# Attention and squared-ReLU feed-forward in one kernel: where the two bursts of a head pair stand among the up products

## The chip, the cores and the metric

The kernel runs on one core of a Trainium2 chip. The metric is the device time of one execution in microseconds, the median of several runs; less is better. Before the change the median of 3 runs is 394.03 us (393.51 to 394.4).

A core has five engines that run side by side and meet only at semaphores. TensorE (PE) multiplies matrices into the eight banks of its result memory (PSUM), VectorE (DVE) and ScalarE (ACT) read those banks, GpSimd (POOL) works between buffers and issues loads, SyncE (SP) issues stores and transposing transfers. In the profile, PEld is the loading of a matmul's stationary operand.

## The reference

Eight batches of 384 tokens pass through attention with 16 query heads and 4 key heads of width 64, then through a feed-forward layer of 1024 to 2048 to 1024 with a squared ReLU:

```python
k = np.repeat(k, group, axis=1)
v = np.repeat(v, group, axis=1)
scores = scale * np.matmul(q, k.transpose(0, 1, 3, 2))
attn = np.exp(scores - max)
attn = attn / (np.sum(attn, axis=-1, keepdims=True) + 1e-09)
attn_out = np.matmul(attn, v)
...
x = attn_out.transpose(0, 2, 1, 3).reshape(B * S, H * D)
h = np.maximum(x @ w_in, 0.0)
out = h * h @ w_out
```

## The kernel before

The kernel is written as a planner in Python. A `Recorder` keeps, for each engine, a clock made from costs written into the code, and appends operations one after the other; at the end `emit` (L116) writes each engine's instructions in that order, with semaphore waits where one engine needs another. So the order on each engine is fixed when the program is built: the planner's clock decides only who goes first, and the chip then waits wherever the planner's clock was too early.

Batches 0 and 1 go through a first loop (L1776 to L1928). Batches 2 to 7 go through the second loop (L1931 to L2014), which the change touches. Per batch b it has two stages.

**Up products.** x times w_in, done as Strassen products (`strassen`, L868): seven products of half size instead of eight. The work is cut into pieces of eight matmuls, four on each half of the array's rows (`zipped`, L836; the matmuls carry L927). There are 28 product tiles, two halves each, so some 57 pieces per batch. Results leave four of the eight banks (4 to 7) by DVE or ACT: copies (L903, L906), additions to an earlier tile (L911), the tile with the ReLU (L898), then the ReLU and square (L812, L820, L824). A bank is used again by the fourth tile after.

**Down products.** The squares times w_out, Strassen again over pairs of row blocks (`stream`, L967; matmuls L971). They are long for odd b (27 us) and short for even b (12 to 14 us). Their results are scaled and added by DVE and ACT (L1126, L1127, L1134) and one addition by POOL (L1169). The first pieces of batch b+1's up products overlap with the last of batch b's down products.

**Attention of the next batch among them.** While batch b is multiplied, batch b+1's attention is done in the gaps of the order, in the other four banks, which are used in two pairs, (0, 1) and (2, 3):

- A score burst, called "sc" (`burst_small`, L464): 2 or 4 matmuls (L471) into one bank pair; ACT then takes the exponential of the whole pair (L481) into a ring of 6 unit slots. A batch has 12 units and 18 score bursts. A slot can be taken again only when the two head pairs that read it are done (L1967).
- A head pair c (8 per batch, `av_halves`, L525): two bursts of 18 matmuls (L539). The first burst ("av") takes a bank pair and holds it, the second ("av2") adds the other halves to it and must not start before the first has ended (`after=(lead,)`, L547). Then DVE reads the pair: a reciprocal (L552), the product into o_sb (L554), and later a maximum (L1506). After every second head pair SP issues a transposing transfer (L559) that turns o_sb into x of batch b+1.
- When all of x is there, DVE forms the sums that batch b+1's Strassen products need (`sums`, L673: four operations at L682 and one at L685). The up products of batch b+1 do not start before that (`ff["b"] in summed`, L1638).

**How the loop chooses.** In each round it collects candidates: the next feed-forward piece ("ffn"), the second burst of an open head pair ("av2"), the first burst of the next ("av"), a spread of a maximum ("top"), a score burst ("sc"). Each has the time from which it can run by the planner's clock, a rank (av2 0, av 1, top 2, sc 3, ffn 5), and whether it is due. The choice is

```python
ready = [x for x in cand if x[3] and x[0] <= now] or [x for x in cand if x[0] <= now]
what = min(ready, key=lambda x: x[1]) if ready else min(cand)
since_av = 0 if what[2] in ("av", "av2") else since_av + (what[2] == "ffn")
```

Inside the up products (`inside`) both kinds of burst are due when four pieces have passed since the last burst, whichever it was (`AV_IN = 4`). A score burst is due when two pieces (`SC_LATE`, batch b+1) or eight (`SC_IN`, batch b+2) have passed since the last score burst. If no due candidate can run, one that is not due may fill the place, and only if nothing at all can run does the planner let PE wait.

Of the kernel before, what the change touches and what calls it, by code (L numbers as in the profile page):

```python
# [171 lines left out]
def bass_gqa_attention__then__ffn_squared_relu_kernel(  # L172
# [32 lines left out]
    R = Recorder(nc)  # L205
# [1415 lines left out]
    ff = dict(b=0, tiles=list(range(EARLY, NFC)), now=[], down=downs(0), carry=None)  # L1621
# [41 lines left out]
    av_open = []  # L1663
    margin = 0.5
    since, AMONG = 9, 2
    AV_IN, SC_LATE, SC_IN = 4, 2, 8
    load_pieces, dma_at, pe_last, LOAD_GAP, TURN_GAP = [], [0.0], [], 2.0, 3.5

    BLOCK, EDGE = 128, 51
# [106 lines left out]
    while ff["b"] < SB:  # L1776
        now = R.clock["tensor"]
# [4 lines left out]
        cand = []  # L1782
        wait = 0.1 if split else 0.0
        if turn_q:
            b, g, w = turn_q[0]
# [5 lines left out]
        if av_q and len(av_open) < 1 + on_halves(av_q[0][0] - 1):  # L1791
            b, c = av_q[0]
# [12 lines left out]
        if sc_q:  # L1805
            b, u = sc_q[0]
# [15 lines left out]
            if ok:  # L1822
# [3 lines left out]
                t = max(R.when(reads=reads) + 1.5 * (b == 2 and u < 9), R.when(writes=[("bank", base + i) for i in range(2)]))  # L1826
                cand.append((t, 4 if beside or loose and b > SB else 2.5 if loose else 0, "sc"))
        early_banks[:] = [i for i in ((6, 7, 0, 1, 2, 3) if sc_q and sc_q[0] == (1, 0) else (6, 7)) if i not in held]
        for n, lane in enumerate(lanes):
            chunks, need, banks, _ = lane[0]  # L1830
            if x_done[0] >= chunks:
                t = R.when(reads=need)
                if banks is not None:
                    if not banks:
                        continue
                    t = max(t, open_bank(banks))
# [4 lines left out]
        if f_head is not None:  # L1841
            chunks, need, banks, piece, *swap = f_head
            if x_done[ff["b"]] >= chunks and not (held and banks and held & set(banks) and isinstance(banks, list)):
                t = max([R.when(reads=need)] + [x() for x in swap])
                if banks:
                    t = max(t, max(open_bank([i]) for i in banks) if isinstance(banks, list) else open_bank(banks))
# [5 lines left out]
        if split:  # L1852
            late = on_halves(ff["b"]) and not (sc_q and sc_q[0][0] == ff["b"] + 1)
            inside = [x for x in cand if x[2] in ("sc", "ffn", "top") or x[2] == "av2" and not on_halves(ff["b"]) or late and (x[2] == "av2" or x[2] == "av" and since >= AMONG * (1 + (ff["b"] >= SB)))]
            if not at_edge or inside and min(inside)[0] <= now + 0.3:
                cand = inside
        if not cand:
            b = next_sum()
# [12 lines left out]
        what = min(ready, key=lambda x: x[1]) if ready else min(cand)  # L1871
# [6 lines left out]
        if what[2] == "turn":  # L1878
            b, g, w = turn_q.pop(0)
# [7 lines left out]
        elif what[2] == "av":  # L1887
            b, c = av_q.pop(0)
            rest = av_halves(b, c, places) if on_halves(b - 1) else av(b, c, spare)
            av_open.append((b, c, rest, next(rest)))  # L1890
        elif what[2] == "av2":
            b, c, rest, _ = av_open.pop(0)
# [34 lines left out]
                R.clock["tensor"] += 0.0 if on_halves(ff["b"] - 1) else 0.1  # L1927
            ff_take(split)  # L1928

    since_av, since_sc = 9, 9  # L1930
    while ff["now"] or ff["tiles"] or ff["down"]:  # L1931
        now = R.clock["tensor"]
        upkeep(now)
        inside = bool(ff["now"])
        cand = []
        head = ff_head(bool(ff["tiles"]))
        if head is not None and not made(head):
            if force():
                continue
            head = None  # L1940
        if head is not None:
            chunks, need, banks, piece, *swap = head
            if x_done[ff["b"]] >= chunks and not (banks and held & set(banks)):
                t = max([R.when(reads=need)] + [x() for x in swap])
                if banks:
                    t = max(t, max(open_bank([i]) for i in banks) if isinstance(banks, list) else open_bank(banks))
                cand.append((t, 5, "ffn", True))
        if av_open:
            cand.append((R.ops[av_open[0][3]]["end"], 0, "av2", since_av >= (AV_IN if inside else 1)))
        if av_q and len(av_open) < 2:  # L1950
            b, c = av_q[0]
            needs = {(b, c // 2 * NJ + j, 3 * (c % 2) + t) for j in range(NJ) for t in range(3)}
            places = [p for p in PAIRS if not held & set(p)]
            if needs <= scored and b in measured and b <= ff["b"] + 1 and b - NXT not in tail_open and places:
                place = min(places, key=lambda p: max(open_bank([i]) for i in p))
                t = max(max(open_bank([i]) for i in place), R.when(reads=av_reads(b, c)))
                cand.append((t, 1, "av", since_av >= (AV_IN if inside else 1)))
        if spread_q:
            pair = min((p for p in PAIRS if not held & set(p)), key=lambda p: max(open_bank([i]) for i in p), default=None)
            if pair:  # L1960
                cand.append((max([R.when(reads=["top_w"]) + 0.8] + [open_bank([i]) for i in pair]), 2, "top", True))
        if sc_q:
            b, u = sc_q[0]
            pieces = later[u]
            tiles = {(b, x, t) for x, c0, n in pieces for t in range(c0 // 128, (c0 + n) // 128)}
            bases = [i for i in (0, 2) if not held & {i, i + 1}]
            if (turned >= b or (b, max(x for _, x, _ in tiles) // (NU // 2)) in turned_h) and b <= ff["b"] + 2 and not (inside and len(ff["now"]) <= 10 and b > ff["b"] + 1) and (b != LEAN or pairs >= 8 * b) and pairs // 2 * NJ + SLOTS[b] > b * NU + max(x for _, x, _ in tiles) and bases:  # L1967
                base = min(bases, key=lambda i: max(open_bank([i + x]) for x in range(2)))
                t = max(R.when(reads=[r for p in pieces for r in score_reads(b, *p)]) + 3.0 * (b > SB + 1), max(open_bank([base + i]) for i in range(2)))
                cand.append((t, 3, "sc", since_sc >= ((SC_LATE if b == ff["b"] + 1 else SC_IN) if inside else 1)))  # L1970
        if not cand:
            if force():
                continue
            b = next_sum()
            if w_q and w_q[0][0]():
                w_q.pop(0)[2]()
            elif b:
                add_sums(b)
            else:
                chores.pop(0)[1]()  # L1980
                if not chores and not halves:
                    turned = queued
            continue
        ready = [x for x in cand if x[3] and x[0] <= now] or [x for x in cand if x[0] <= now]
        what = min(ready, key=lambda x: x[1]) if ready else min(cand)
        since_av = 0 if what[2] in ("av", "av2") else since_av + (what[2] == "ffn")
        since_sc = 0 if what[2] == "sc" else since_sc + (what[2] == "ffn")
        if what[2] == "av":
            b, c = av_q.pop(0)
            rest = av_halves(b, c, [place])  # L1990
            av_open.append((b, c, rest, next(rest)))
        elif what[2] == "av2":
            b, c, rest, _ = av_open.pop(0)
            widest_of(b, c - 3)
            next(rest, None)
            pairs += 1
            if b >= FAST:
                wide_q.append((b, c))
                if c == 7:
                    m_q.append((b, lambda b=b: widest_of(b)))  # L2000
            if c % 2 == 1:
                o_wait.append((b, c // 2))
                if c == 7:
                    turn_o_waiting()
        elif what[2] == "top":
            n, then = spread_q.pop(0)
            top_spread(n, pair)
            then()
        elif what[2] == "sc":
            b, u = sc_q.pop(0)  # L2010
            burst_small(b, pieces, base)
            scored |= tiles
        else:
            ff_take(bool(ff["tiles"]))  # L2014
# [31 lines left out]
```

## Time and profile before

| | us |
|---|---|
| median of 3 runs | 394.03 (393.51 to 394.4) |
| the profiled execution | 394.68 |
| its span, first to last instruction | 392.6 |
| first loop, to the first up products of batch 2 | 0 to 128.2 |
| up products of batches 2, 3, 4, 5, 6 (with attention) | 24.8, 24.9, 24.4, 25.0, 24.5 |
| down products after them | 13.7, 27.0, 14.2, 26.8, 12.2 |
| up and down products of batch 7 (no attention left) | 20.3 and 26.6 |

The stage borders are those of this trace: the first matmul of L927 of a batch to its last, and the stretch up to the next batch's first. Over the whole span DVE is busy 79%, ACT 69% and POOL 37%. In lists of instructions one row may stand for several of the same kind, "x36"; the time of a row reaches from its first start to its last end, so that matmuls which overlap are not to be added. The granted clock of TensorE is 1.0 throughout.

### The profile page before, as it was taken

The page shows a single profiled execution, that of the slowest core. Times are in us where ns is not written, and L with a number is a line of the kernel's source. Part 1 is how long each engine was busy: PE and PEld are TensorE (multiplying, and loading weights), DVE is VectorE, ACT ScalarE, POOL GpSimd, SP SyncE. Part 2 cuts the span into 40 slices and gives each one's busy share as a digit, 9 for nine tenths or more (in the row PEclk, how much of TensorE's full clock was granted, in tenths as well). Part 3 has the DMA queues.
Part 4 walks back from the last instruction along what each step waited for, and adds up shares of the span by engine and source line. Part 5 has one row for each costly group of instructions (what it writes and reads, how often), then busy time and mean ns, then how long its engine had stood idle before and what let it go on. Part 6 is the DMA issues. An engine that isn't in the chain of part 4 may idle for free. (4 is left out here: it accounts for less than half of the span.)

```text
span 392.6 us, 15577 instructions
## 1 busy us (share of the span) xinstructions
PE 386.4 (98%) x6987; PEld 305.3 (78%) x6990; DVE 309.0 (79%) x645; ACT 272.1 (69%) x397; POOL 143.6 (37%) x167
## 2 busy tenths in 40 slices
PE   8899999999999999999999999999999999999997
PEld 6565674455555899899988999899988899899643
DVE  4589788899989988888886678797885688856642
ACT  6848998789845897868882587878782297435511
POOL 7765420044002563466422154526401145225210
PEclk9999999999999999999999999999999999999999
DMA  9999999996339875884798316877722222120013
GB/s 176 179 197 154 206 202 178 160 258 103 42 78 131 182 104 75 126 161 79 99 133 172 120 25 83 123 139 94 69 64 86 102 46 23 48 83 4 28 68 122
DMA packets 95635, 44.40 MB, mean 113 GB/s; under 512 B 75984, under 2 KB 89552, under 8 KB 95568
## 3 DMA queue, kind: packets, MB, share of 16 engines
q0 software_dynamic: 36672, 17.44, 35.7%
q1 hardware_dynamic: 58080, 25.39, 32.2%
q8 instruction: 55, 0.90, 1.0%
q10 hardware_dynamic: 816, 0.57, 0.5%
q14 instruction: 12, 0.10, 0.1%
HBM read 35.65 MB, written 12.58 MB: 123 GB/s over the span
## 5 line engine op out<-in xcount | busy, mean ns | idle before, releaser
L481 ACT ACTIVATE expT<-ps 128x1024 bf16<-128x1024 f32 (+1 forms) x124 | 121.1, 1015 | 24.7 <-PE ps L471 24.3
L971 PE MATMUL ps<-w_out_sb,h2T 64*128 64x512 f16 x512 | 94.5, 376 | 0.0
L927 PE MATMUL ps<-xT,w_in_sb 64*128 64x192 f16 x1152 | 84.3, 243 | 0.3 <-DVE y_sb L1134 0.2
L927 PEld LDWEIGHTS ps<-xT,w_in_sb 64*128 64x128 f16 x1152 | 70.5, 94 | 3.0 <-PE ps L927 0.7
L824 POOL TENSOR_TENSOR h2T<-hr 128x384 f16<-128x384 f32 x55 | 44.8, 835 | 53.7 <-ACT hr L812 53.6
L927 PE MATMUL ps<-s_all,wx 64*128 64x192 f16 x768 | 51.8, 242 | 0.0
L471 PE MATMUL ps<-qT,kT 64*128 64x256 bf16 (+2 forms) x336 | 51.3, 323 | 0.5 <-DVE qT L442 0.2
L812 ACT ACTIVATE hr<-hr,bits 128x384 f32<-128x384 f32 x72 | 42.6, 608 | 11.1 <-DVE hr L911 10.7
L971 PE MATMUL ps<-area,xT 64*128 64x512 f16 x256 | 50.1, 376 | 0.0
L971 PEld LDWEIGHTS ps<-w_out_sb,h2T 64*128 64x128 f16 (+1 forms) x512 | 38.0, 94 | 14.8 <-DVE hr L898 0.4
L911 DVE TENSOR_TENSOR hr<-ps,hr 128x384 f32<-128x384 f32 x72 | 39.3, 555 | 8.4 <-PE ps L927 5.1
L927 PEld LDWEIGHTS ps<-s_all,wx 64*128 64x128 f16 x768 | 43.7, 94 | 1.2
L1126 ACT ACTIVATE y_sb<-ps,bits 128x512 f32<-128x512 f32 (+2 forms) x23 | 15.3, 669 | 40.4 <-PE ps L971 31.2
L1134 DVE SCALAR_TENSOR_TENSOR y_sb<-ps,bits,y_sb 128x512 f32<-128x512 f32 (+1 forms) x36 | 26.3, 745 | 21.1 <-PE ps L971 13.2
L635 PE MATMUL ps<-xT,w_in_sb 64*128 64x384 bf16 x448 | 41.6, 323 | 0.4 <-DMA w_in_sb<-in_moe_w_in_dram 0.2
L539 PE MATMUL ps<-v_aug,expT 64*128 64x65 bf16 x1680 | 41.8, 190 | 0.1
L539 PEld LDWEIGHTS ps<-v_aug,expT 64*128 64x128 bf16 x1680 | 38.4, 94 | 1.9 <-DVE o_sb L554 0.3
L635 PEld LDWEIGHTS ps<-xT,w_in_sb 64*128 64x128 bf16 x448 | 22.2, 94 | 15.0 <-issue 1.3
L927 PE MATMUL ps<-xT,wx 64*128 64x192 f16 x384 | 32.6, 242 | 0.0
L927 PE MATMUL ps<-s_all,w_in_sb 64*128 64x192 f16 x384 | 32.5, 242 | 0.0
L971 PE MATMUL ps<-area,h2T 64*128 64x512 f16 x128 | 31.9, 376 | 0.0
L903 ACT COPY hr<-ps 128x384 f32<-128x384 f32 x33 | 15.5, 481 | 23.3 <-PE ps L927 22.7
(152 smaller groups left out, 746.1 us busy)
## 6 DMA issues: line engine op xcount, KB each, us to landing
out_dram<-y_sb SPq DMA_DIRECT2D x45, 256.0 KB, 2.5
w_in_sb<-in_moe_w_in_dram POOLq DMA_DIRECT2D x8, 512.0 KB, 15.1
w_out_sb<-in_moe_w_out_dram POOLq DMA_DIRECT2D x4, 1024.0 KB, 30.9
q_st<-in_q_dram POOLq DMA_DIRECT2D x19, 192.0 KB, 5.1
q_st<-in_q_dram POOLq DMA_DIRECT2D x4, 384.0 KB, 25.5
k_st<-in_k_dram POOLq DMA_DIRECT2D x6, 192.0 KB, 4.5
k_st<-in_v_dram POOLq DMA_DIRECT2D x5, 192.0 KB, 4.8
wx<-in_q_dram POOLq DMA_DIRECT2D x2, 384.0 KB, 6.7
```

The costliest lines, as they stand in the source:

```text
L471: mm = pe.matmul(ps[:, base + x, m * wide:(m + 1) * wide], kT[at(b)][64 * x:64 * x + 64, u, :], q_cols(b, u // NJ, x, c0, c0 + wide))
L481: R.add("scalar", lambda e: e.activation(dst, src, AF.Exp, scale=0.125), reads=keys, writes=[("expT", slot(b, u), t) for u, _, _ in pieces ...
L539: m = pe.matmul(ps[:, p[x], n * DP:n * DP + D + 1], w, v_aug[b % 2][r, g * NJ + j, 0:D + 1], start=(n + j + y == 0), stop=(n + j + y == 2 ...
L635: m = pe.matmul(bank(4 + xs[x])[:, 0:S], w_in_sb[r, kc, c * 128:(c + 1) * 128], xT[b % NXT][r, kc, :], start=(phase < 2 and kc == 0), stop ...
L812: R.add("scalar", lambda e, val=val, to=to: e.activation(val, val, AF.Relu, scale=to), reads=[("hr", r)] + by, writes=[("hr", r)], cost=0. ...
L824: n = R.add(eng, lambda e, dst=dst, two=two: e.tensor_tensor(dst, two, two, ALU.mult), reads=[("hr", r)], writes=keys, cost=0.77 if other ...
L903: R.add("scalar", lambda e: e.copy(hr[r][:, :], src), reads=[("bank", at)], writes=[("hr", r)], cost=0.45, after=hr_read.pop(r, ()))
L911: R.add("vector", lambda e: e.tensor_tensor(hr[r][:, :], src, hr[r][:, :], ALU.add), reads=[("bank", at), ("hr", r)], writes=[("hr", r)], ...
L927: return lambda pe: pe.matmul(bank(at)[:, f * h:f * h + h], w[r, kc, c:c + 128], m[r, kc, :], start=(prod in (1, 5, 2) and y + f + kc == 0 ...
L971: return lambda pe: pe.matmul(bank(p.at)[:, 0:512], p.a(k, r), p.w(k, r), start=start, stop=stop, skip_group_check=True)
L1126: R.add(eng, lambda e: e.activation(y_sb[y][:, c0:c1], bank(at)[:, c0:c1], AF.Copy, scale=gs[g]) if eng == "scalar" else e.tensor_scalar(y ...
L1134: R.add("vector", lambda e: e.scalar_tensor_tensor(y_sb[z][:, c0:c1], bank(at)[:, c0:c1], gs[g], y_sb[y][:, c0:c1], ALU.mult, ALU.add), re ...
```

## The change

When a head pair is open and the next one can run, its second burst now waits for seven pieces instead of four, and the first burst of the next pair follows directly behind it. A score burst may not come between the fourth piece after a burst and the next one while this holds. If the next pair's banks or exponentials are not ready at seven pieces, the second burst goes alone at ten. If no next pair can run within 3 us by the planner's clock, the old spacing of four holds.

```diff
-    AV_IN, SC_LATE, SC_IN = 4, 2, 8
+    AV_IN, AV_JOINT, EARLY_SC, SC_LATE, SC_IN = 4, 7, 4, 2, 8
...
-    since_av, since_sc = 9, 9
+    since_av, since_sc, behind = 9, 9, False
...
-        if av_open:
-            cand.append((R.ops[av_open[0][3]]["end"], 0, "av2", since_av >= (AV_IN if inside else 1)))
+        place, joint, behind_at = None, False, 0.0
...
-                cand.append((t, 1, "av", since_av >= (AV_IN if inside else 1)))
+                cand.append((t, 1, "av", since_av >= (AV_IN if inside else 1) and not av_open or behind))
+                joint, behind_at = inside and t <= now + 3.0, t
+        if av_open:
+            cand.append((R.ops[av_open[0][3]]["end"], 0, "av2", since_av >= AV_JOINT and behind_at <= now + 0.1 or since_av >= AV_JOINT + 3
+                         if joint else since_av >= (AV_IN if inside else 1)))
...
-                cand.append((t, 3, "sc", since_sc >= ((SC_LATE if b == ff["b"] + 1 else SC_IN) if inside else 1)))
+                cand.append((t, 3, "sc", not (joint and since_av >= EARLY_SC) and since_sc >= ((SC_LATE if b == ff["b"] + 1 else SC_IN) if inside else 1)))
...
+        behind = what[2] == "av2"
```

No instruction is added or taken away: the same bursts, pieces, reads of banks and transfers are put in another order, on PE and, since the planner places them after their producers, on DVE, ACT, POOL and SP too. The first loop and its order are untouched. Two head pairs may have been open before as well (`len(av_open) < 2`); what is new is that a pair of banks is held for seven pieces, that a first burst is due directly after a second one, and that otherwise it is due only while no head pair is open.

## The prediction

> **What bounds the kernel now.** I read the page's busy times first, then the busy times by stage, then the chain of waits through one stage, then the timeline at the few places where TensorE stood still.
>
> ```profile
> PE 386.4 (98%) x6987; PEld 305.3 (78%) x6990; DVE 309.0 (79%) x645; ACT 272.1 (69%) x397; POOL 143.6 (37%) x167
> ```
>
> ```profile
> 128.20:153.00 24.80, 24.71 (x682) 23.05 (x677) 22.04 (x44) 22.02 (x34) 15.30 (x17) 1.00 0.65 117
> ...
> 166.70:191.60 24.90, 24.90 (x729) 24.21 (x726) 21.66 (x50) 19.15 (x28) 14.87 (x16) 1.00 0.62 111
> ...
> 218.60:243.00 24.40, 24.40 (x736) 23.68 (x735) 20.16 (x43) 17.71 (x28) 9.71 (x12) 1.00 0.37 72
> 243.00:257.20 14.20, 14.20 (x166) 12.43 (x163) 11.66 (x26) 13.15 (x19) 6.23 (x7) 1.00 0.88 126
> 257.20:282.20 25.00, 24.76 (x737) 23.85 (x734) 21.50 (x46) 18.54 (x28) 11.65 (x14) 1.00 0.66 98
> ...
> 309.00:333.50 24.50, 24.50 (x737) 23.76 (x735) 20.17 (x43) 17.71 (x28) 9.81 (x12) 1.00 0.30 60
> ```
>
> The columns are the stage, its length, then the busy time of PE, PEld, DVE, ACT and POOL. The reader is to see that PE has almost no idle time where the change acts. The five up stages with attention in them have 0.09, 0, 0, 0.24 and 0 us of it, 0.33 in all. DVE stands at 81 to 89% of them, so it has slack, but not much. The number of matmuls stays the same, so a new order can win only what PE loses between them, and can lose whatever new wait it makes.
>
> Is a burst itself cheaper when it stands beside another? The chain of waits through the up products of batch 5, with one row of batch 6 (start, length, what, how many matmuls):
>
> ```profile
> 258.74 0.29 PE ps L539 x18
> 259.03 0.33 PE ps L927 x8
> 259.36 0.56 PE ps L539 x36
> ...
> 261.24 0.28 PE ps L539 x18
> 261.52 0.22 PE ps L471 x2
> ...
> 263.28 0.27 PE ps L539 x18
> ...
> 310.46 0.57 PE ps L539 x36
> ```
>
> A single burst takes 0.27 to 0.29, a piece 0.33, a score burst 0.22. In two places the kernel before already has a second burst directly in front of the next pair's first: 36 matmuls, 0.56 and 0.57 us. That is two single bursts.
>
> **The change part by part.** *Joined bursts.* One join replaces two stays between pieces by one. From the rows, its worth lies between 2 x 0.29 - 0.56 = 0.02 us won and 0.57 - 2 x 0.27 = 0.03 lost. I take 0, since 0.28 is the middle of the single rows and exactly half of 0.56. How many joins are there? Four up stages have 14 or 15 bursts whole inside (252 and 270 matmuls of 18, below), batch 2's 11.5; I count 4 joins a stage, 20 in all (worked out below), so the ends are 0.4 won and 0.6 lost.
>
> Weighed against a rule: by the Trainium skill, TensorE: Matmul & The Clock Gate, section "Wait — 56ns, not 53.3ns?", a warm matmul costs its columns at 2.4 GHz and about 2.5 ns, which for nine pairs of 65 columns on the two row halves would be an estimated 0.27 us a burst. By that, the 0.01 to 0.02 us above it could be a price of entry that a join pays once, some 0.2 to 0.4 us over 20 joins. The trace speaks against it, since the joined 36 carry the same surplus twice.
>
> *The spacing, and how many joins come about.* Score bursts and head pairs share two bank pairs. The rows of one ordinary second burst and the score burst behind it, from the timelines of PE, DVE and ACT:
>
> ```profile
> 261.07 0.45 PE L539 MATMUL ps<-v_aug,expT 64*128 64x65 bf16 x18
> 261.36 0.38 PE L471 MATMUL ps<-qT,kT 64*128 64x512 bf16 x2
> ...
> 261.56 0.20 DVE L552 RECIPROCAL bits<-ps 128x6 f32<-128x6 f32 x1
> 261.79 0.56 DVE L554 TENSOR_TENSOR o_sb<-ps,bits 128x384 f16<-128x384 f32 x1
> ...
> 261.78 1.02 ACT L481 ACTIVATE expT<-ps 128x1024 bf16<-128x1024 f32 x1 [0.35 <-PE ps L471]
> ```
>
> The bank pair of the second burst is free at 261.79 + 0.56 = 262.35, 1.28 us after the burst's start. A score burst occupies its pair from 261.36 to 261.78 + 1.02 = 262.80, 1.44 us. Before, the score burst goes to the other pair at once. Joined, the other pair is held by the next head pair, so the score has to wait for the pair just read. A joined period is 7 x 0.33 + 0.56 + 0.22 = 3.09 us; one score burst fits (1.28 + 1.44 = 2.72), a second one (4.16) doesn't.
>
> ```profile
> 128.20:153.00 24.80, 5.04 (x207) 4.37 (x201) 1.00 0.65 117
> 166.70:191.60 24.90, 6.38 (x252) 5.95 (x253) 1.00 0.62 111
> 257.20:282.20 25.00, 6.56 (x270) 6.03 (x270) 1.00 0.66 98
> ...
> 128.20:153.00 24.80, 4.99 (x36) 1.73 (x36) 1.00 0.65 117
> 257.20:282.20 25.00, 3.47 (x24) 1.13 (x24) 1.00 0.66 98
> ```
>
> These are the stages for L539 alone (three rows) and for L471 alone (two). Batch 5's stage has 24 score matmuls, which are 9 bursts (six of 2, three of 4), for units 6 to 11; their slots open only as head pairs end. Units 0 to 5 are scored before the stage, so pairs 0 to 3 can join. Pair 4 needs three more units, four score bursts, and two joined periods give only two. There the next pair isn't ready, the old spacing of four returns, the scores catch up, and the last pairs join again. Counted through the rules of the loop, the eight pairs end at some 50 to 56 of the 57 pieces, where they now reach to the last (4 x 15 = 60, the last burst lies among the first down matmuls). So x of the next batch is complete about 1 to 3 us earlier (4 to 10 pieces of 0.33). This alone is worth nothing, because behind the up products follow 12 us or more of down products that don't need x.
>
> *The waits that are there now.* Two are near enough to be touched. The timelines of PE, DVE and POOL at the start of batch 5:
>
> ```profile
> 257.35 0.33 PE L927 MATMUL ps<-xT,w_in_sb 64*128 64x192 f16 x2
> 257.92 0.24 PE L927 MATMUL ps<-xT,w_in_sb 64*128 64x192 f16 x1 [0.24 <-DVE y_sb L1134]
> ...
> 252.06 2.00 DVE L682 TENSOR_TENSOR s_all<-xT 128x768 f16<-128x768 f16 x1
> 254.10 0.56 DVE L682 TENSOR_TENSOR s_all<-s_all,xT 128x768 f16<-128x768 f16 x1
> ...
> 255.51 0.21 DVE L685 TENSOR_SCALAR bits<-bits 128x1 f32<-128x1 f32 x1
> ...
> 257.03 0.75 DVE L1134 SCALAR_TENSOR_TENSOR y_sb<-ps,bits,y_sb 128x512 f32<-128x512 f32 x1
> ...
> 251.71 1.92 POOL L1242 COPY area<-h2T 128x2048 f16<-128x2048 f16 x1
> ```
>
> Two pairs of L927 start at 257.35, at 0.33 / 4 = 0.08 us a pair; the next is due at 257.35 + 0.16 = 257.51 and comes at 257.92. The loss is 0.41 us. DVE is late with L1134 because the four sums (L682) of batch 5 stood in front of it, and the first of them took 2.00 instead of 0.56 while POOL's copy ran from 251.71 to 253.63. With x there 1 to 3 us earlier the sums leave DVE earlier, so I take this loss as gone: -0.41, with 0 as the other end.
>
> The rule behind that row is in the Trainium skill, SBUF — State Buffer, section "SBUF: two separate sides": a DVE operation with two SBUF inputs and a GpSimd operation that reads SBUF exclude each other for the whole instruction. The trace agrees (2.00 against 0.56), and it speaks against this change too, since sums that move by 1 to 3 us may meet another POOL operation; that would cost up to the same 1.44 us on DVE.
>
> The other place is in batch 2's stage:
>
> ```profile
> 134.23 0.95 PE L539 MATMUL ps<-v_aug,expT 64*128 64x65 bf16 x36
> 135.03 0.24 PE L927 MATMUL ps<-xT,w_in_sb 64*128 64x192 f16 x1
> ...
> 134.73 0.33 PEld L539 LDWEIGHTS ps<-v_aug,expT 64*128 64x128 bf16 x18 [0.19 <-PE ps L539]
> ```
>
> Here 36 matmuls take 0.80 instead of 0.56: both bursts are of one pair, and the second waits for the end of the first. The planner had nothing else to run, and the change leaves that fallback as it is. I take 0, with -0.24 as the other end.
>
> *New waits.* The planner puts a score behind the reading of its banks by its own clock, 0.22 + 0.48 = 0.70 us for L552 and L554 in the code, against 262.35 - 261.56 = 0.79 in the rows. PE may arrive up to 0.09 us early, once in a joined period, 20 times: 0 to 1.8 us. Pieces come in steps of 0.33, so most arrivals are later than the bank; I take 0.2. The cover is that step: if each of the 20 met the full 0.09, all 1.8 would show.
>
> *Other queues.* The moved bursts issue no transfers themselves; the turning of o_sb on SP (L559) and the loads on POOL come at other moments, with a cost of 0 as long as x has the down products in front of it.
>
> *Sum.* 0 - 0.41 + 0 + 0.2 = -0.2 us on the profiled execution: span 392.4, its time 394.68 - 0.2 = 394.5. That execution lies 0.65 above the median of the runs, so **the forecast is 393.8 us**.
>
> **The rivals.**
>
> *Slower, x comes too late.* The score bursts of batch 3 are themselves the limit of its attention: batch 2's stage has 36 score matmuls and only 207 of L539 (rows above), and the rest spills into the short down products. The margin:
>
> ```profile
> 165.36 0.21 DVE L685 TENSOR_SCALAR bits<-bits 128x1 f32<-128x1 f32 x1
> ...
> 166.87 0.32 PE L927 MATMUL ps<-xT,w_in_sb 64*128 64x192 f16 x2
> ```
>
> The last of the sums ends at 165.57 and the up products start at 166.87, 1.30 us later (batch 5: 255.72 to 257.19, 1.47). The change bars a score for pieces 4 to 6 of a joined period, 0.99 us each time. Three such bars on the way to the last pair put x 2.97 us later; from 1.30 us on PE waits one for one: 2.97 - 1.30 = 1.67, 395.7 us. For it: scores, not bursts, set the pace there. Against it: the bar holds only while the next pair is ready, so when scores are short it lifts.
>
> *Slower, scores behind the only free bank pair.* All 20 arrivals meet the 0.09: 1.8 instead of 0.2, so 395.4 us. For it: DVE at 86% in batch 5's stage (21.50 of 25.00). Against it: there is no such wait in the stages now.
>
> *Faster, everything loose is won.* Both known waits go (0.65), no new one comes, and a join wins its 0.02 (0.4): 394.03 - 1.05 = 393.0 us. For it: the joined order leaves PE busy 0.56 us while DVE, which has just got the 0.79 us of L552 and L554, receives nothing new. Against it: the fallback at 134.23 is unchanged and the joined rows show no gain.
>
> *It hardly joins.* Were the next pair seldom ready, the order would nearly be the old one: 394.0 us.
>
> **How the numbers follow.** Forecast 0.44 (own range 393.3 to 394.8), x too late 0.22, scores behind the bank 0.12, everything won 0.16, hardly joins 0.06. A measurement of this kernel can tell about 0.2% (0.8 us) from no change: under 393.2 is faster, over 394.8 slower. Faster gets 0.15 of the rival and 0.05 of the forecast's low end, 0.20; slower gets both slow rivals and 0.03 of the forecast's high end, 0.37; the same the remaining 0.43. The range runs from the fast rival's 393.0, widened by 0.1 for the spread of the median, to the later of the slow ones: 392.9 to 395.8.
>
> **What would show it.** Right: rows of L539 x36 at 0.56 to 0.57 with seven pieces (2.31 us) around them in about half of each stage, idle PE in the up stages still near 0.3, the gap at the start of batch 5 gone, the last L539 of a stage 1 to 3 us before the first down product. Wrong: idle PE in front of L471 put down to DVE o_sb L554 (scores behind the bank); idle PE at the start of batch 3, 5 or 7 with L682 or L685 as releaser (x too late); an x36 row clearly under 0.54 (joins pay); an L682 of 1 to 2 us in a new place.

## The result, and the profile after

| | before | after |
|---|---|---|
| median of 22 runs each, us | 394.33 (393.51 to 395.5) | 395.39 (394.73 to 395.93) |
| the profiled execution | 394.68 | 395.11 |
| its span | 392.6 | 393.0 |

The ratio is 1.0026, 95% interval 1.0019 to 1.0033: the change costs about 1.06 us. The spans differ by 0.4 us only, because the profiled execution of before reached batch 2 late, in the first loop, which the change doesn't touch: its first L927 of batch 2 starts at 126.93, that of after at 126.17. So the traces are compared from that matmul on. From there to the end before takes 265.71 us and after 266.82, 1.11 more, close to what the medians say. The table ahead of the prediction ends the first loop at 128.2 and starts batches 4 and 6 at 218.6 and 309.0; the first L927 stand at 126.93, 218.20 and 308.68, and everything from here on is counted from those.

This table holds, for every profiled kernel, the time from the first L927 of batch 2 to the first L927 of a later batch, and to the end, as a difference to before (us). For batch 3 after it is (166.71 - 126.17) - (166.87 - 126.93) = 0.60, printed 0.59 since it is made from unrounded starts.

```
                                       batch 3     4      5      6      7    end
before, the times themselves             39.94  91.27 130.26 181.75 218.80 265.71
after                                    +0.59  +0.50  +0.53  +0.45  +0.47  +1.10
joined in all batches but 6              +0.64  +0.55  +0.57  +0.44  +0.42  +0.38
joined in batch 6 alone                   0.00   0.00   0.00   0.00  +0.03  +0.66
no bar for scores                        +1.39  +1.66  +1.69  +2.34  +2.35  +6.82
POOL's addition of batch 6 on DVE        +0.54  +0.45  +0.47  +0.35  +0.36  +0.67
sums of batch 7 first                    +0.54  +0.45  +0.48  +0.35  +0.36  +0.34
before, copy behind the sums              0.00   0.00   0.00  -0.40  -0.40  -0.40
four pieces between joins                +0.54  +0.36  +0.40  +1.67  +1.67  +2.31
joined in batch 2 alone                  +0.53  +0.39  +0.38  +0.33  +0.33  +0.31
sums first and copy behind the sums      +0.70  +0.61  +0.63  +0.51  +0.53  +0.50
the same, four pieces                    +0.54  +0.35  +0.39  +0.21  +0.21  +0.19
the same, seven, old spacing in batch 2  +0.01  +0.14  +0.17  +0.04  +0.06  +0.02
before, sums of batch 7 later            +0.01  +0.01  +0.01   0.00   0.00  -0.01
```

Each row is one trace. Eight kernels have the joined order of bursts in batch 2 as after has it, and still differ there, from 0.53 to 0.70 at batch 3. So a difference of up to 0.17 us in batch 2 is not read as an effect. Behind batch 2, kernels with the same order agree to 0.05 us a batch.

Two steps make the row of after: 0.59 in batch 2 and 0.63 between the first up product of batch 7 and the end.

**The last step.** What PE waited for after 125 us (in all, times, longest), before and after:

```profile
PE ps L927 <- DVE y_sb L1134: 0.2, 1, 0.2
```

```profile
PE ps L927 <- DVE hr L911: 0.5, 1, 0.5
PE ps L927 <- DVE y_sb L1344: 0.2, 1, 0.2
```

The wait of before is the one at the start of batch 5. The second of after stands at 128.35, near the start of batch 2's up products; the run with the sums first, which has the same order on PE, doesn't have it, so it isn't counted to the change. The timelines of PE, DVE and POOL around the first, after:

```profile
350.29 0.50 PE L927 MATMUL ps<-s_all,wx 64*128 64x192 f16 x8 [0.49 <-DVE hr L911]
...
343.37 0.29 DVE L713 TENSOR_REDUCE bits<-ps 128x1 f32<-128x128 f32 x1 [1.56 <-PE ps L709]
...
343.96 0.54 DVE L682 TENSOR_TENSOR s_all<-xT 128x768 f16<-128x768 f16 x1
344.54 0.56 DVE L682 TENSOR_TENSOR s_all<-s_all,xT 128x768 f16<-128x768 f16 x1
345.01 0.74 DVE L1134 SCALAR_TENSOR_TENSOR y_sb<-ps,bits,y_sb 128x512 f32<-128x512 f32 x1
345.68 0.55 DVE L682 TENSOR_TENSOR xT<-xT 128x768 f16<-128x768 f16 x1
346.14 1.62 DVE L682 TENSOR_TENSOR s_all<-xT,s_all 128x768 f16<-128x768 f16 x1
...
348.36 1.40 DVE L1134 SCALAR_TENSOR_TENSOR y_sb<-ps,bits,y_sb 128x512 f32<-128x512 f32 x2
349.68 1.01 DVE L911 TENSOR_TENSOR hr<-ps,hr 128x384 f32<-128x384 f32 x2
...
345.84 1.51 POOL L1169 TENSOR_TENSOR y_sb<-y_sb 128x512 f32<-128x512 f32 x1 [12.69 <-DVE y_sb L1134]
```

The same place before:

```profile
341.13 0.55 DVE L682 TENSOR_TENSOR s_all<-xT 128x768 f16<-128x768 f16 x1
...
342.66 0.55 DVE L682 TENSOR_TENSOR s_all<-xT,s_all 128x768 f16<-128x768 f16 x1
343.13 0.28 DVE L713 TENSOR_REDUCE bits<-ps 128x1 f32<-128x128 f32 x1
```

Read the rows of after from the back. PE waits for L911, and L911 stands behind two L1134, which stand behind L685 and the sums. The fourth sum took 1.62 instead of 0.55 us, and it overlaps L1169 on POOL (345.84 to 347.35). L1169 was released by the L1134 at 345.01, which now stands between the sums. The sums start 1.48 us ahead of batch 7's first L927 (345.44 - 343.96) instead of 4.60 (345.73 - 341.13), 3.12 us later, because the planner now places them behind L713, and DVE idles 1.56 us there for PE's L709. Before, sums come first and L713 after them. On the chip they did not wait for x itself: its last transfer (L559) was issued at 336.2 and landed 2.8 us later, some 5 us before the sums start. In the kernel before it was issued at 335.2.

**Why the sums are later.** The chain of waits through batch 6's up products, before (its first row of L927 in the stage, and the last burst of the eight pairs) and after:

```profile
308.93 0.08 PE ps L927
...
334.03 0.07 PE ps L539 x2
```

```profile
308.54 0.08 PE ps L927
...
310.12 0.55 PE ps L539 x34
310.68 2.32 PE ps L927 x56
313.00 0.55 PE ps L539 x34
...
320.55 2.64 PE ps L927 x64
323.19 0.28 PE ps L539 x18
...
335.24 0.07 PE ps L539 x2
```

The first pairs are joined as meant, 36 matmuls in 0.55 us (two of them in neighbouring rows where the chain has x34) with seven pieces (2.32 us) between. Then the scored units run out: thirteen pieces pass between the end of one pair's burst at 318.29 and the next at 323.02, the last eight of them (2.64 us) with no score burst either, and ACT's exponential (L481) that ends at 322.66 comes just before the burst. Single bursts follow, and the last pair is closed among the down products. A row of the chain begins where the one before it ends, so the stage is measured by PE's timeline: from the first L927 to the start of the last matmul of L539 before takes 333.91 - 308.68 = 25.23 us, after 335.12 - 308.38 = 26.74, 1.51 more. The stage's rows for L539 alone count it too, before and after:

```profile
308.68:334.51 25.83, 7.11 (x288) 6.53 (x288) 1.00 0.29 57
```

```profile
308.38:333.35 24.97, 5.55 (x235) 5.12 (x237) 1.00 0.24 58
```

53 matmuls, about three bursts of 18, have left the stage. Its shorter length is no gain: these bursts stand among the down products now.

**The other places.** At the start of batch 5 (timelines of PE, DVE and POOL, after):

```profile
257.12 0.54 PE L927 MATMUL ps<-xT,w_in_sb 64*128 64x192 f16 x3
257.51 0.32 PE L927 MATMUL ps<-xT,w_in_sb 64*128 64x192 f16 x2
...
255.01 0.54 DVE L682 TENSOR_TENSOR s_all<-xT 128x768 f16<-128x768 f16 x1
...
258.82 1.88 POOL L1242 COPY area<-h2T 128x2048 f16<-128x2048 f16 x1
```

These are single matmuls on one half of the rows, one every 0.08 us, while the other half is still with L971. Three of them from 257.12 are due to be followed at 257.12 + 3 x 0.08 = 257.36, and the next comes at 257.51: 0.15 lost, against 0.41 before. The sums start later, at 255.01, and POOL's copy comes after them.

In batch 2, two bursts are long (timeline of PE, after; behind it a burst of before among the same down products):

```profile
146.92 0.45 PE L539 MATMUL ps<-v_aug,expT 64*128 64x65 bf16 x18
147.28 0.25 PE L927 MATMUL ps<-xT,w_in_sb 64*128 64x192 f16 x1
...
153.91 0.55 PE L539 MATMUL ps<-v_aug,expT 64*128 64x65 bf16 x18
154.34 0.37 PE L971 MATMUL ps<-w_out_sb,h2T 64*128 64x512 f16 x1
```

```profile
154.16 0.45 PE L539 MATMUL ps<-v_aug,expT 64*128 64x65 bf16 x15
...
154.55 0.37 PE L971 MATMUL ps<-area,h2T 64*128 64x512 f16 x1
```

The first holds PE for 147.28 - 146.92 = 0.36 instead of 0.28 us. The second holds it for 154.34 - 153.91 = 0.43, but among the down products a burst held it for 154.55 - 154.16 = 0.39 before as well. So they explain 0.08 + 0.04 = 0.12 us. More of the step is work that has moved. The rows for L471 alone, from the first L927 of batch 2 to that of batch 3, before and after:

```profile
126.93:166.87 39.94, 8.49 (x58) 3.56 (x56) 1.00 0.78 123
```

```profile
126.17:166.71 40.54, 8.54 (x62) 3.01 (x60) 1.00 0.78 123
```

After has four score matmuls more here and fewer in batch 3; a score burst holds PE for 0.22 us. Some of that comes back: the table's row falls to 0.50 by batch 4.

### The profile page after: what moved, and what is told of

It reads as the page before. It is cut to its first block, busy times and chain, and to the rows that moved or that the text cites. A ratio compares the mean times of both kernels' runs of the same rounds, so it can differ in the third digit from the quotient of the medians.

```text
span 393.0 us, 15586 instructions
## 1 busy us (share of the span) xinstructions
PE 387.9 (99%) x6987; PEld 291.1 (74%) x6990; DVE 310.3 (79%) x647; ACT 272.7 (69%) x394; POOL 145.1 (37%) x168
## 4 chain that ended last, share of the span: by engine, by line
PE 91%; DVE 5%; ACT 2%; DMA 1%; issue 0%
PE ps L927 28%; PE ps L971 27%; PE ps L635 9%; PE ps L471 7%; PE ps L539 7%; PE ps L1319 5%; PE ps L1026 2%; PE ps L497 2%; ACT expT L481 2%; DMA xT<-o_sb 1%; PE ps L598 1%; PE ps L1406 1%; DVE s_all L682 1%; DVE area L1274 1%; PE ps L573 1%; DVE y_sb L1134 1%
## 5 line engine op out<-in xcount | busy, mean ns | idle before, releaser
L481 ACT ACTIVATE expT<-ps 128x1024 bf16<-128x1024 f32 (+1 forms) x124 | 121.8, 1019 | 26.0 <-PE ps L471 25.5
L971 PE MATMUL ps<-w_out_sb,h2T 64*128 64x512 f16 x512 | 95.1, 376 | 0.0
L927 PE MATMUL ps<-xT,w_in_sb 64*128 64x192 f16 x1152 | 82.6, 243 | 0.3 <-DVE y_sb L1344 0.2
L927 PEld LDWEIGHTS ps<-xT,w_in_sb 64*128 64x128 f16 x1152 | 71.2, 94 | 3.3 <-DVE y_sb L1344 0.5
L471 PE MATMUL ps<-qT,kT 64*128 64x256 bf16 (+2 forms) x336 | 50.7, 326 | 0.5 <-ACT expT L481 0.4
L927 PE MATMUL ps<-s_all,wx 64*128 64x192 f16 x768 | 50.2, 243 | 0.5 <-DVE hr L911 0.5
L971 PE MATMUL ps<-area,xT 64*128 64x512 f16 x256 | 50.0, 376 | 0.0
L971 PEld LDWEIGHTS ps<-w_out_sb,h2T 64*128 64x128 f16 (+1 forms) x512 | 37.0, 94 | 16.1 <-DVE hr L898 0.4
L911 DVE TENSOR_TENSOR hr<-ps,hr 128x384 f32<-128x384 f32 x72 | 39.5, 556 | 11.1 <-PE ps L927 7.3
L927 PEld LDWEIGHTS ps<-s_all,wx 64*128 64x128 f16 x768 | 44.0, 94 | 2.0 <-DVE hr L911 0.7
L539 PE MATMUL ps<-v_aug,expT 64*128 64x65 bf16 x1680 | 40.1, 190 | 0.1
L1134 DVE SCALAR_TENSOR_TENSOR y_sb<-ps,bits,y_sb 128x512 f32<-128x512 f32 (+1 forms) x36 | 26.3, 744 | 16.6 <-PE ps L971 10.8
L1126 ACT ACTIVATE y_sb<-ps,bits 128x512 f32<-128x512 f32 (+2 forms) x20 | 13.2, 666 | 37.6 <-PE ps L971 28.6
L539 PEld LDWEIGHTS ps<-v_aug,expT 64*128 64x128 bf16 x1680 | 37.2, 94 | 2.0 <-DVE o_sb L554 0.3
L903 ACT COPY hr<-ps 128x384 f32<-128x384 f32 x38 | 17.9, 480 | 24.4 <-PE ps L927 23.9
L1169 POOL TENSOR_TENSOR y_sb<-y_sb 128x512 f32<-128x512 f32 x8 | 10.8, 1356 | 61.1 <-DVE y_sb L1134 61.1
L927 PE MATMUL ps<-s_all,w_in_sb 64*128 64x192 f16 x384 | 33.3, 243 | 0.0
L635 PEld LDWEIGHTS ps<-xT,w_in_sb 64*128 64x128 bf16 x448 | 21.3, 94 | 15.3 <-DVE hr L648 0.8
L971 PE MATMUL ps<-area,h2T 64*128 64x512 f16 x128 | 32.4, 376 | 0.0
```

Source lines behind the costliest of these rows:

```text
L471: mm = pe.matmul(ps[:, base + x, m * wide:(m + 1) * wide], kT[at(b)][64 * x:64 * x + 64, u, :], q_cols(b, u // NJ, x, c0, c0 + wide))
L481: R.add("scalar", lambda e: e.activation(dst, src, AF.Exp, scale=0.125), reads=keys, writes=[("expT", slot(b, u), t) for u, _, _ in pieces ...
L539: m = pe.matmul(ps[:, p[x], n * DP:n * DP + D + 1], w, v_aug[b % 2][r, g * NJ + j, 0:D + 1], start=(n + j + y == 0), stop=(n + j + y == 2 ...
L635: m = pe.matmul(bank(4 + xs[x])[:, 0:S], w_in_sb[r, kc, c * 128:(c + 1) * 128], xT[b % NXT][r, kc, :], start=(phase < 2 and kc == 0), stop ...
L903: R.add("scalar", lambda e: e.copy(hr[r][:, :], src), reads=[("bank", at)], writes=[("hr", r)], cost=0.45, after=hr_read.pop(r, ()))
L911: R.add("vector", lambda e: e.tensor_tensor(hr[r][:, :], src, hr[r][:, :], ALU.add), reads=[("bank", at), ("hr", r)], writes=[("hr", r)], ...
```

## The experiments

Theory 1: the loss in batch 7 comes from the place of the sums on DVE and the POOL operation that meets them, and the joined bursts themselves cost nothing. The rival: the joined order itself costs, through late pairs, banks and scores. All ratios are to the kernel before, run on the same chip, with 95% intervals.

**Where the loss sits.** Joined everywhere but in batch 6's up products:

```diff
-cand.append((t, 1, "av", since_av >= (AV_IN if inside else 1) and not av_open or behind))
-joint, behind_at = inside and t <= now + 3.0, t
+cand.append((t, 1, "av", since_av >= (AV_IN if inside else 1) and not (av_open and ff["b"] != 6) or behind and ff["b"] != 6))
+joint, behind_at = inside and t <= now + 3.0 and ff["b"] != 6, t
```

> The joined order in the up products of batches 2 to 5, the old order in those of batch 6. Theory (late sums): in the changed kernel the last head pair of batch 7 ends later than before, the sums of batch 7 run 2.8 us later, the last of them meets a POOL addition (1.62 instead of 0.55 us), DVE is late for the banks and PE waits 0.65 us at 350 us. Then this kernel loses that wait: sums of batch 7 done before the up products of batch 7 start, no idle PE near 350 us, and a time about 0.4 us over the kernel before instead of 1.06. Rival (each joined stage costs the same, 0.2 us): about 0.85 us over.

Measured 394.37 against 394.25 us, ratio 0.9993 (0.9979 to 1.0007). The wait in batch 7 is gone: the trace ends 0.38 above before instead of 1.10.

The counterpart, joined in batch 6 alone (the same edit with `== 6`):

> The joined order in the up products of batch 6 alone. Late sums: the wait near 350 us is there, L682 with one row over 1 us, and the time is 0.65 us over the kernel before. Rival (each joined stage costs the same): 0.2 us over.

Measured 394.39, ratio 1.0001 (0.9988 to 1.0013). Its trace agrees with before to 0.03 us up to batch 7 and then loses 0.63, with the same wait for L911 of 0.5 us. The medians of these two say less than their traces (0.38 and 0.66 us above before): the intervals end at 0.3 and 0.5 us above. So they place the loss, but the traces and not the times measure it.

Joined in batch 2 alone (`== 2`):

> The joined order in the up products of batch 2 alone. By the losses of PE between the matmuls (0.38 us more in this stage and the down products behind it than before): 0.4 us over the kernel before, and nothing new in the other stages. If batch 2's stage counts for nothing: 0.

Measured 394.31 against 393.89, ratio 1.0012 (1.0003 to 1.0021), and the trace ends 0.31 above before. Both steps of after have their own stage: batch 2 some 0.3 to 0.4 us once batch 3 has given some of it back, batch 6 into 7 some 0.6.

**What makes the wait in batch 7.** The addition L1169 of batch 6 moved from POOL to DVE:

```diff
-R.add("gpsimd", lambda e: e.tensor_tensor(y_sb[z], y_sb[z], y_sb[y], ALU.add),
-      reads=[("y", y), ("y", z)], writes=[("y", z)], cost=1.28)
+R.add("vector" if b == 6 else "gpsimd", lambda e: e.tensor_tensor(y_sb[z], y_sb[z], y_sb[y], ALU.add),
+      reads=[("y", y), ("y", z)], writes=[("y", z)], cost=0.6 if b == 6 else 1.28)
```

> The changed kernel with the addition of L1169 for batch 6 on DVE instead of POOL. If the exclusion between POOL's addition and the last sum makes the wait: no L682 over 0.6 us at 346 us, the wait near 350 us shrinks from 0.65 to under 0.25 us, 0.4 to 0.6 us less than the changed kernel. If lateness alone is enough: the wait stays at 0.5 us or more, since DVE has 0.6 us more to do there.

Measured 394.75, ratio 1.0012 (0.9997 to 1.0027). DVE's timeline, and PE's only wait after 125 us:

```profile
345.85 0.69 DVE L1169 TENSOR_TENSOR y_sb<-y_sb 128x512 f32<-128x512 f32 x1
...
346.93 0.55 DVE L682 TENSOR_TENSOR s_all<-xT,s_all 128x768 f16<-128x768 f16 x1
```

```profile
PE ps L927 <- DVE hr L911: 0.2, 1, 0.2
```

The long sum is gone, but DVE has the addition itself, 0.69 us; the wait falls from 0.5 to 0.2. The collision is part of the loss; the rest stays with the late place, or with the addition that DVE now has.

Then the sums alone: the time for which the planner holds them back after x, shorter for batch 7, with PE's order as in after:

```diff
-+ (3.3 if b > SB + 1 else 3.3 if b > SB else 2.0) <= now + 0.3:
++ (2.0 if b == 7 else 3.3 if b > SB + 1 else 3.3 if b > SB else 2.0) <= now + 0.3:
```

> The changed kernel with the order of PE untouched; on DVE alone the four sums of batch 7 stand ahead of the reading of the spread maximum (L713) instead of behind it. Late sums: the sums end before POOL's addition begins (no L682 over 0.6 us near 346 us), no idle PE near 350 us, 0.6 us less than the changed kernel, so 0.4 us over the kernel before. If the order of the bursts on PE is itself what costs, nothing changes: 1.06 us over.

Measured 394.36 against 393.89, ratio 1.0009 (1.0000 to 1.0017). Timelines of DVE and POOL:

```profile
342.25 0.55 DVE L682 TENSOR_TENSOR s_all<-xT 128x768 f16<-128x768 f16 x1
...
343.78 0.55 DVE L682 TENSOR_TENSOR s_all<-xT,s_all 128x768 f16<-128x768 f16 x1
...
346.33 1.26 POOL L1169 TENSOR_TENSOR y_sb<-y_sb 128x512 f32<-128x512 f32 x1 [12.65 <-DVE y_sb L1134]
```

No sum is long, L1169 comes 2.00 us after the last of them has ended (343.78 + 0.55 = 344.33), and the profile lists no wait of PE after 125 us. With the same bursts in the same places on PE, batch 7 costs nothing (+0.36 at its start, +0.34 at the end). POOL's copy L1242 of this batch still stands behind L1169, as in after, so its place isn't what cost. The late pair is harmless as long as the sums still go ahead of L713.

The reverse, in the kernel before: batch 7's sums held back for 4.5 instead of 3.3 us, which puts them behind L713 and leaves PE's order alone:

```diff
++ (4.5 if b == 7 else 3.3 if b > SB + 1 else 3.3 if b > SB else 2.0) <= now + 0.3:
```

> The kernel before, PE's and ACT's order unchanged, with batch 7's four sums placed behind L713, L1525 and L1527 on DVE and L1169 ahead of the copy L1242 on POOL, as the kernel after has them; an addition L1134 follows the sums here instead of standing between them, so that L1169, which needs it, cannot run beside them. Theory 1 (the collision with POOL makes the loss): L685 ends about 2 us later, but the sums take 0.55 us each and PE does not wait: 0 to 0.1 us above before. Rival (being placed behind L713 is enough): PE waits for L911 at the start of batch 7, 0.5 us above before.

Measured 393.69 against 394.08, ratio 0.9992 (0.9982 to 1.0002), and the trace ends within 0.01 us of before:

```profile
342.42 0.54 DVE L682 TENSOR_TENSOR s_all<-xT 128x768 f16<-128x768 f16 x1
...
343.94 0.55 DVE L682 TENSOR_TENSOR s_all<-xT,s_all 128x768 f16<-128x768 f16 x1
344.41 0.74 DVE L1134 SCALAR_TENSOR_TENSOR y_sb<-ps,bits,y_sb 128x512 f32<-128x512 f32 x1
...
345.23 1.26 POOL L1169 TENSOR_TENSOR y_sb<-y_sb 128x512 f32<-128x512 f32 x1 [11.97 <-DVE y_sb L1134]
```

Here L1134 follows the sums, so L1169 cannot run beside them. Being placed behind L713 costs nothing by itself, at least this early: the sums start 344.95 - 342.42 = 2.53 us ahead of batch 7's first L927, in after 1.48. The kernel after has besides an addition between the sums, the collision with L1169, and x that is later; with the collision away and the addition on DVE, 0.67 - 0.36 = 0.31 of the 0.63 stayed, and this rest was not divided further.

**The wait at the start of batch 5.** In the kernel before, POOL's copy L1242 waits for the last sum of the next batch:

```diff
-writes=[("h2x", b), ("h2x", b - 2)] + X_OVER, cost=2.0), True))
+writes=[("h2x", b), ("h2x", b - 2)] + X_OVER, cost=2.0, after=(R.writer[("S", 2)],)), True))
```

> The kernel before, all orders the same, with one more wait: POOL's copy L1242 waits for the last of the sums of the next batch. If the exclusion between POOL's copy and the first sum (2.00 us) is what makes PE wait at the start of batch 5: all four L682 of batch 5 at 0.55 us, the wait of 0.4 us there shrinks to 0.2 or less, 0.2 to 0.4 us under the kernel before. If not: no change there, 0.

Measured 393.62 against 393.89, ratio 0.9995 (0.9986 to 1.0003); the trace gains 0.40 in batch 5 and nowhere else. Timelines of DVE and POOL:

```profile
251.41 0.54 DVE L682 TENSOR_TENSOR s_all<-xT 128x768 f16<-128x768 f16 x1
...
253.54 1.89 POOL L1242 COPY area<-h2T 128x2048 f16<-128x2048 f16 x1 [2.46 <-DVE s_all L682]
```

The sum that took 2.00 beside the copy takes 0.54, and the wait of 0.41 is gone. The prediction's reading of that wait was right, and it goes without touching the order of the bursts.

**The spacing.** No bar for score bursts (`not (joint and since_av >= EARLY_SC) and` left out):

> The changed kernel without the bar on score bursts from the fourth piece on. If the bar is what makes the last pair late: last pair of each batch where it was before, about 0 us over the kernel before. If it is the single free bank pair that makes the scores late (my theory of the lateness): in the stage of batch 6 the last pair still ends among the down products, the wait near 350 us stays, 0.6 to 1.1 us over.

Measured 400.14, ratio 1.0134 (1.0109 to 1.0159). From the first L927 of batch 6 to the start of the last matmul of L539 it takes 336.83 - 310.10 = 26.73 us (after: 335.12 - 308.38 = 26.74; before: 333.91 - 308.68 = 25.23). So the bar is not what makes the last pair late. Of the 6.82 us that its trace loses, 2.35 arise before batch 7, most of them in batches 2 and 5, and were not followed. The larger part, 4.47, is lost in the same place as in after, since two sums meet POOL (timeline of DVE, then PE's longest wait):

```profile
347.91 1.63 DVE L682 TENSOR_TENSOR xT<-xT 128x768 f16<-128x768 f16 x1
349.46 2.24 DVE L682 TENSOR_TENSOR s_all<-xT,s_all 128x768 f16<-128x768 f16 x1
```

```profile
PE ps L927 <- DVE hr L911: 2.7, 1, 2.7
```

Four pieces between joins instead of seven (`AV_JOINT = 4`):

> The changed kernel with four pieces instead of seven between joined bursts. If it is the spacing that makes the last pair late: last burst of a stage right at the first down products, about 1 us earlier than in the changed kernel, sums of batch 7 done by 345 us, no wait near 350 us, 0.3 to 0.5 us over the kernel before. If the joins themselves cost: still about 1.06 us over, since it has as many.

Measured 396.42 against 393.89, ratio 1.0069 (1.0052 to 1.0086): slower than after. The last pair is indeed less late (335.51 - 309.64 = 25.87), so seven pieces make 0.87 of the 1.51 us. This did not help batch 7, which loses 2.31 - 1.67 = 0.64 as in after: its sums start at 345.23, 1.46 us ahead of its first L927 at 346.69, and the last of them takes 1.62. And the sums of batch 5 now start at 253.01 instead of 255.01 and meet the copy that after had missed (timelines of PE, DVE and POOL):

```profile
258.68 0.24 PE L927 MATMUL ps<-xT,w_in_sb 64*128 64x192 f16 x1 [1.31 <-DVE y_sb L1134]
...
253.01 1.99 DVE L682 TENSOR_TENSOR s_all<-xT 128x768 f16<-128x768 f16 x1
...
252.66 1.92 POOL L1242 COPY area<-h2T 128x2048 f16<-128x2048 f16 x1
```

This went against what was expected, and it speaks for theory 1: the time follows the place of the sums and what they meet, not how late the last pair is.

**Both mends together.** After with the sums of batch 7 first and the copy behind the sums (the two diffs above):

> The kernel after with batch 7's four sums (L682) placed ahead of L713 on DVE and POOL's copy (L1242) held back until the last sum of the next batch; PE's order is unchanged. Theory 1 (what the change loses is the sums' place on DVE and the POOL operations they meet; the joined bursts cost nothing): the wait at the start of batch 7's up products stays away as in the run with the sums first, the rest of the wait at the start of batch 5 (0.14 us) goes too, so 0.2 us above the kernel before. Rival (the joined order of bursts and scores itself costs): no better than the run with the sums first, 0.35 to 0.5 us above before.

Measured 394.64 against 394.08, ratio 1.0011 (0.9998 to 1.0025). The profile lists no wait of PE after 125 us; the trace ends 0.50 above before, with 0.70 already lost in batch 2, where the run with the sums first lost 0.54 with the same bursts. That is above the 0.2 expected, and within the rival's 0.35 to 0.5. Holding the copy back won nothing here: in batch 5 this run gains 0.12 and the run with the sums first alone 0.13. The copy was behind the sums already, so the 0.15 at the start of batch 5 has another cause, which was not tried; an addition L1134 stands between the sums there too.

The same with four pieces:

> Joined bursts with four pieces between instead of seven, and both mends of the run before (sums of batch 7 ahead of L713, copy behind the sums). The four-piece order lost 2.3 us by its trace, of which 1.53 is the wait at the start of batch 5 (a sum took 1.99 us beside POOL's copy) and 0.66 at the start of batch 7. Theory 1: both go, and 0.1 to 0.4 us above before remains. Rival (four pieces are too few for the banks and the scores, the order itself costs): still 1.5 us or more above before.

Measured 394.15, ratio 0.9999 (0.9986 to 1.0013). Against the run with four pieces and no mends 2.1 us are gone by the trace (2.31 to 0.19). The bursts of batch 5 stand in another order here as well, so this is not a pure test of the mends, but of the rival's 1.5 us nothing remains.

The same with seven pieces, and the old spacing in batch 2:

> The first kernel of this set with the old spacing in batch 2's up products, joined in batches 3 to 6. Theory 1: the 0.38 us that the joined order loses in batch 2's up and down products go, so 0.2 - 0.38 = 0.2 us below before (0.0 to 0.3 below). Rival (each joined stage costs): 0.2 to 0.4 us above before.

Measured 394.09, ratio 1.0003 (0.9990 to 1.0016), trace +0.02. The joined order in batches 3 to 6, with both collisions away, ends where before does. But before still has its own wait at batch 5; against before with the copy behind the sums the joined order is 0.02 + 0.40 = 0.42 slower by trace. 0.13 of it arise in batch 3 and 0.27 in batch 5, of which 0.15 is the wait at its start, as in after. So theory 1 is shown for batch 7, and the rival is not excluded for some 0.4 us in batches 3 to 5 and for what batch 2 loses. Before with the copy behind the sums is the fastest kernel by trace, but its time is not told from before's.

## Why the prediction was partly right and partly wrong

The direction was wrong: 0.2 us faster was forecast, 1.06 slower came. The measured 395.39 lies inside the range, but only because the range reached up to the slow rivals, and neither of them happened as it was told.

- **Joined bursts cost nothing: right for the burst, open for the order.** 36 matmuls take 0.55 us. But with both collisions away the joined order of batches 3 to 6 is still 0.42 us above before with the copy behind the sums, and 0.27 of that is not explained.
- **"The eight pairs end at some 50 to 56 of the 57 pieces ... x of the next batch is complete about 1 to 3 us earlier": wrong, and this is the step that failed.** I saw that the next pair would not be ready after four pairs, but let the old four pieces stand for that wait. Pairs are worked off early at seven pieces each, then thirteen pieces pass with no burst of a pair, and what remains runs at the old four. The last burst of batch 6's stage comes 1.51 us later, and the last transfer of x is issued 1.3 us later against batch 7's first L927 (345.44 - 336.2 = 9.2 ahead of it, before 345.73 - 335.2 = 10.5).
- **"This alone is worth nothing, because ... 12 us or more of down products": wrong cover.** The down products hide x, but the sums are placed on DVE by the planner's clock, and a later x moved them past L713, with an addition between them, 3.12 us later. Batch 7 lost 0.63 us by it. The place on DVE's queue was the cover, and it was near its edge.
- **The stall at the start of batch 5, -0.41: its cause right, its size not.** 0.15 of it stayed. It shrank because the sums came later and POOL's copy behind them, not because x came earlier.
- **New waits of scores, 0.2: not there.** PE has no wait for L554 in front of a score burst after 125 us.
- **The fallback in batch 2, 0: right in that no wait went; but batch 2's stage was given no cost and has 0.3 to 0.4 us.** 0.12 of it are two long bursts, and a score burst of 0.22 us was brought forward from batch 3. Why the bursts are long, and where the rest lies, was not tried.
- **The rival "x comes too late" is what happened, at another place.** It was placed at batch 3, with L685 ending before the up products as the point of decision. In batch 3 L685 ends at 167.00 and the up products start at 166.71 without a wait: L685 isn't what the first matmuls need. It decided at batch 7, through L1134 and L911 behind the sums.

The prediction's sentence that moved sums may meet another POOL operation named the mechanism. It gave no term to it. By the Trainium skill, SBUF — State Buffer, section "SBUF: two separate sides", a DVE operation with two SBUF inputs and a GpSimd operation that reads SBUF exclude each other for the whole instruction. The traces agree: 1.62 beside L1169, 1.99 and 2.24 beside the copy, 0.55 alone.

## What to carry to other kernels

When an order is changed, follow the last producer of the next stage and not the first joins: what is worked off early leaves a gap, and the last one may come later. A cover of 12 us on one engine says nothing about the place that the consumer gets in another engine's queue; write down what stands next in that queue, and what that would release. Where two operations hold each other up as these did, a shift of one or two us in either direction can make or remove a collision (batch 5's sums met the copy in before and with four pieces, not in after), and such a stall can be mended by an explicit order, worth 0.40 us by the trace here.

## What the hardware showed beside it

In the run without the bar, PE waited 2.7 us at batch 7's start, from 351.5 to 354.2, and around its end the granted clock fell. The windows of that run (length, busy time of PE, PEld, DVE, ACT and POOL, granted clock, DMA share, GB/s):

```profile
353.50:355.50 2.00, 1.28 (x18) 1.18 (x20) 1.13 (x3) 0.41 (x2) 0.00 (x0) 0.67 0.71 262
355.50:358.50 3.00, 3.00 (x54) 2.84 (x50) 1.12 (x2) 1.21 (x4) 1.61 (x2) 0.65 0.03 5
358.50:362.00 3.50, 3.50 (x90) 3.50 (x88) 2.56 (x5) 2.59 (x5) 1.69 (x3) 1.00 0.00 0
```

54 matmuls in 3.00 us at 0.65, against 90 in 3.50 at 1.00. So one wait of 2.7 us cost 6.82 - 2.35 = 4.47 us from batch 7's start to the end, more than the wait itself. It need not happen: of this kernel's six runs three, the profiled one among them, had a mean granted clock of 0.996 over the execution and took 400.34 to 401.7 us, and three had 1.0 and took 398.36 to 399.94. The Trainium skill, TensorE: Matmul & The Clock Gate, section "Part 1: The HAM clock gate", has the clock halved after an idle window of about 3.4 us; here a wait of 2.7 us was enough, and the windows show 0.65 to 0.67. Waits of up to 1.31 us, in the run with four pieces, left the clock at 1.00.
